# Attention with a memory, then a mixture of experts: loads moved to ScalarE's queue, the sum of the attended values split by head, and a new table of offsets

## The chip, the cores and the metric

The kernel runs on one core of one Trainium2 chip. A core has TensorE (PE: matrix products and transposes, results in eight PSUM banks), VectorE (DVE), ScalarE (ACT), GpSimd (POOL) and SyncE (SP), which mostly issues DMAs. Each engine takes its instructions strictly in the order in which they were written into its queue. The metric is the device time in microseconds of one execution; less is better.

## What is computed

```python
# q, k, v: B=4, H=8, S=576, D=64;  M_prev (B,H,D,D), z_prev (B,H,D), beta (H)
scores = where(causal, -1e9, q @ k^T / sqrt(D));  a = softmax(scores)
local = a @ v
q_p = where(q > 0, q, exp(q) - 1) + 1
mem_out = (q_p @ M_prev) / (q_p . z_prev + 1e-6)
g = sigmoid(beta)                       # one number a head
attn = g * mem_out + (1 - g) * local
x = attn as (B*S, H*D)                  # 2304 tokens x 512
logits = x @ w_gate + modality_bias[modality_id]
e_idx = argmax(logits);  gate_w = softmax(logits)[e_idx]
for e in range(8):                      # F = 1024
    out[e_idx == e] = gate_w * (relu(x @ w1[e]) @ w2[e])
```

Everything is float32.

## The kernel before

A product in float32 accuracy is made of three products of rounded parts: an operand is split into a high part (an `fp32r` copy, by ScalarE) and the rest (value minus copy, by VectorE or GpSimd), so `qh`/`ql`, `kh`/`kl`, `pth`/`ptl`, `vhl`, `xh`/`xl`, `hh`/`hlo`, `w1h`/`w1l` in the traces.

**Attention** goes by pairs of heads (16 pairs, four to a batch of 576 tokens). For a pair: q and k are loaded (`load_t`, `qn`, `kn`), transposed on TensorE (L554), split, and partly copied by DMA to other partitions (`qs`, `ks`, `kls`, L568/L569). Per head: scores on TensorE (L657), mask and row maximum by a VectorE instruction (L669), exponent on ScalarE (L675), transposes (L684), split (L701 ScalarE, L703 VectorE), product with v (L715, L720). A head's attended values stand in PSUM in two halves, partitions 0 to 63 and 64 to 127, that must be added; the function `av` does that into `ot` by way of the buffer `avt`. Then `memory` (L758 to L774: the product with `M_prev`, in the buffer `mz`, loaded by `load_m`), and `combine` (L783 to L801: transposes `ot` back, scales, adds, into the row buffer `xb`, which is stored as x).

**Routing** follows each batch: `gate` makes logits; `route` is a run of small VectorE instructions (steps e0 to e7, L852 to L917) on 128x40 and 128x8 values with three little TensorE products between them, and five indirect DMAs (L920) that GpSimd issues, which scatter (token number, weight) into three tables `tbl`; `rank` (L932 to L945) finds the fullest expert (after batch 0) and the second (after batch 2).

**Experts** work in slots of 256 or fewer rows: `fetch` reads the slot's token numbers from the tables (`idr`, L1009, merged on VectorE, L999/L1000), gathers rows of x by indirect DMA (`xg`, L1016); `slot` transposes them (L1042), makes the first product (L1064), the relu and its split (L1073, L1075), the second product (L1086), scales (L1093) and scatters rows of the output (L1024). `load_w` loads weights (L978) and splits them (L985 ScalarE, L989). The fullest expert's weights are loaded while attention still runs, into the buffers `xg` and `osb`, and three slots of it (EARLY = 3) are run between pairs of the last three batches. `leftovers` lists what the last batch added.

**What sets the order.** No engine chooses at run time. Every step is given to a list scheduler, `Plan`, with its engine, a cost in ns, the buffers it reads and writes and a priority: a number n that counts heads, plus the offset that the table `EARLIER` holds for its stage and engine. Stages are q, k, v, ld (loads), sc (scores), pt (transposes of the probabilities), av, m (memory), c (combine), g, r (route and rank), w (the fullest expert's weights), f and e (its fetches and slots), f1, e1, f2, e2, w1, w2, l, l2 (what follows attention), con (the gate's constants), bet, tab, warm. The scheduler runs its own clock with those costs; among the steps of an engine that could start within `WINDOW` ns of the earliest it emits the one with the lowest priority. A changed cost or offset changes the order of instructions everywhere after it.

The start: TensorE fills the time before data with products of ones (`warm`), q of the first pair is transposed, then k; GpSimd sets up masks and constants; VectorE makes `wgs` and `modf` from the loaded gate constants (L470 to L472) and step e0 of the first routing when the order says so.

## Time and profile before

| what | value |
|---|---|
| median of three runs | 554.32 us (549.8 to 556.81) |
| profiled execution | 550.81 us, its span 549.1 us |
| mean granted clock of TensorE | 0.966 of full speed |
| busy, of the span | PE 497.9 us, DVE 330.5, ACT 329.0, POOL 251.9 |
| DMA traffic, mean | 128 GB/s |

The profiled execution's time is the number that a run reports; the span is what the trace covers of it, 1.7 us less. Shares are of the span. Attention takes about the first 310 us, the last routing is at 337 us, and after it there is almost only TensorE work. "idle before" in a row is how long the engine had nothing running before that instruction, and the name behind the arrow is what its wait ended with.

### The profile page before, as it was taken

The numbers are of one execution on the slowest core, as the hardware profiler recorded it, in microseconds if no ns is written. First come the engines' busy times: TensorE is split into PE (matmuls) and PEld (weight loads), VectorE is DVE, ScalarE is ACT, GpSimd is POOL, SyncE is SP. The second block draws the span as 40 slices with busy tenths as digits, with TensorE's granted clock in tenths as the row PEclk, the third lists the DMA queues.
The fourth block names the chain that finished last, engine by engine and source line by source line (L and its number), as shares of the span: only waits on it lengthen the run. The fifth ranks groups of instructions, "written<-read, shape, count | busy, mean of one in ns | idle before, by whom it ended". The sixth has DMA issues, their size and how long they took to land. (4 is left out here: it accounts for less than half of the span.)

```text
span 549.1 us, 10861 instructions
## 1 busy us (share of the span) xinstructions
PE 497.9 (91%) x3420; PEld 445.1 (81%) x3420; DVE 330.5 (60%) x1066; ACT 329.0 (60%) x923; POOL 251.9 (46%) x257
## 2 busy tenths in 40 slices
PE   8898899987899889979898999769999999999992
PEld 8787888875787778869897898769897987989891
DVE  3788788897798988988878336653315512313010
ACT  4798898986999979979298244333325513222110
POOL 8462984656788768865761062350030004010100
PEclk9799899999899989989899999979999999999997
DMA  5888887988777997953740025474036203000100
GB/s 96 189 206 169 206 201 182 231 189 154 192 176 198 238 189 191 220 164 95 180 110 3 20 61 180 78 233 146 18 96 182 83 19 88 29 19 21 40 0 36
DMA packets 97101, 70.43 MB, mean 128 GB/s; under 512 B 73936, under 2 KB 74320, under 8 KB 97042
## 3 DMA queue, kind: packets, MB, share of 16 engines
q1 hardware_dynamic: 93330, 59.99, 45.2%
q0 software_dynamic: 3712, 9.72, 5.8%
q8 instruction: 28, 0.46, 0.4%
q14 instruction: 31, 0.25, 0.2%
HBM read 32.36 MB, written 10.16 MB: 77 GB/s over the span
## 5 line engine op out<-in xcount | busy, mean ns | idle before, releaser
L675 ACT ACTIVATE P<-P,nm 128x576 f32<-128x576 f32 (+4 forms) x160 | 88.5, 558 | 9.1 <-DVE nm L669 6.0
L1024 POOL DMA_INDIRECT out_dram<-osb,ids x19 | 18.9, 997 | 156.0 <-ACT osb L1093 115.3
L1064 PE MATMUL pa<-xh,w1h 128*128 128x256 f32 (+2 forms) x288 | 84.4, 293 | 2.6 <-ACT xh L1050 2.6
L1064 PE MATMUL pa<-xl,w1h 128*128 128x256 f32 (+2 forms) x288 | 83.4, 290 | 0.5 <-DVE xl L1052 0.3
L1064 PE MATMUL pa<-xh,w1l 128*128 128x256 f32 (+2 forms) x288 | 83.1, 288 | 0.0
L1075 DVE SCALAR_TENSOR_TENSOR hlo<-pa,hh 128x256 fp32r<-128x256 f32 (+1 forms) x72 | 29.8, 416 | 69.8 <-ACT hh L1073 69.7
L703 DVE TENSOR_TENSOR ptl<-pa,pth 128x512 fp32r<-128x512 f32 (+1 forms) x128 | 65.6, 564 | 3.0 <-ACT pth L701 2.4
L1073 ACT ACTIVATE hh<-pa 128x256 fp32r<-128x256 f32 (+1 forms) x80 | 29.0, 367 | 61.1 <-PE pa L1064 54.2
L669 DVE CUSTOM_DVE_ANT_0 P<-pa,maskw 128x320 f32<-128x320 f32 (+3 forms) x160 | 62.2, 427 | 4.2 <-PE pa L657 3.5
L684 PE MATMUL pa<-ident,P 128*128 128x128 f32 x320 | 57.6, 285 | 4.0 <-ACT P L675 3.7
L657 PE MATMUL pa<-ks,qs 128*128 128x192 f32 (+3 forms) x186 | 55.5, 329 | 5.9 <-ACT avt L735 2.9
L1086 PE MATMUL pa<-w2h,hh 128*128 128x512 f32 (+1 forms) x152 | 60.4, 397 | 0.0
L701 ACT ACTIVATE pth<-pa 128x512 fp32r<-128x512 f32 (+1 forms) x128 | 57.0, 511 | 5.0 <-PE pa L684 4.4
L1086 PE MATMUL pa<-w2l,hh 128*128 128x512 f32 (+1 forms) x152 | 59.6, 392 | 0.0
L1064 PEld LDWEIGHTS pa<-xh,w1h 128*128 128x128 f32 x288 | 55.6, 193 | 3.4 <-ACT xh L1050 2.9
L1064 PEld LDWEIGHTS pa<-xl,w1h 128*128 128x128 f32 x288 | 55.6, 193 | 1.2 <-DVE xl L1052 0.9
L1086 PE MATMUL pa<-w2h,hlo 128*128 128x512 f32 (+1 forms) x144 | 56.5, 392 | 0.0
L1064 PEld LDWEIGHTS pa<-xh,w1l 128*128 128x128 f32 x288 | 55.5, 193 | 0.0
L1093 ACT ACTIVATE osb<-pa,ids 128x512 f32<-128x512 f32 (+1 forms) x19 | 13.1, 687 | 68.4 <-PE pa L1086 63.1
L657 PE MATMUL pa<-kls,qs 128*128 128x192 f32 (+3 forms) x186 | 49.2, 295 | 0.4 <-DMA kls<-kl 0.4
L684 PEld LDWEIGHTS pa<-ident,P 128*128 128x128 f32 x320 | 40.4, 147 | 6.3 <-ACT P L675 6.0
L684 PE MATMUL pa<-swp,P 128*128 128x128 f32 x160 | 39.5, 287 | 6.1 <-DVE kl L617 2.5
(234 smaller groups left out, 1198.9 us busy)
## 6 DMA issues: line engine op xcount, KB each, us to landing
ks<-kh SPq DMA_DIRECT2D x62, 144.0 KB, 3.0
kls<-kl SPq DMA_DIRECT2D x62, 144.0 KB, 3.4
raw<-in_moe_w_dram SPq DMA_DIRECT2D x32, 256.0 KB, 3.5
qn<-in_q_dram SPq DMA_DIRECT2D x32, 144.0 KB, 4.3
kn<-in_k_dram SPq DMA_DIRECT2D x32, 144.0 KB, 4.2
qs<-qh SPq DMA_DIRECT2D x31, 144.0 KB, 2.6
qs<-ql SPq DMA_DIRECT2D x31, 144.0 KB, 2.7
vn<-in_v_dram SPq DMA_DIRECT2D x32, 128.0 KB, 3.0
```

Source lines behind the costliest of these rows:

```text
L657: nc.tensor.matmul(t.ap[0:m, o:o + z - x], lhsT=l[:, QS[j]:QE[j]], rhs=r[:, x:z], start=(i == 0), stop=(i == len(terms) - 1))
L669: nc.vector.tensor_tensor_reduce(out=pj[:, x:z], in0=t.ap[0:m, o:o + z - x], in1=mk, scale=-1.0, scalar=nm if x else 3.0e38, op0=ALU.add, ...
L675: g.op("ACT", act_ns(w, False, 2), lambda pj=pj, nm=nm, den=den, w=w: nc.scalar.activation(out=pj[:, 0:w], in_=pj[:, 0:w], func=AF.Exp, sc ...
L684: nc.tensor.transpose(t[:, o:o + P], prow[c % NPB][j][:, kb * P:(kb + 1) * P], swp if j == kb else ident)
L701: g.op("ACT", act_ns(n), lambda t=t, o=o, n=n: nc.scalar.activation(out=hi[:, o:o + n], in_=t.ap[:, 0:n], func=AF.Copy), r=[t], w=[("ph_", ...
L703: g.op("DVE", dve_ns(n), lambda t=t, o=o, n=n: nc.vector.tensor_tensor(out=lo[:, o:o + n], in0=t.ap[:, 0:n], in1=hi[:, o:o + n].bitcast(F3 ...
L1024: g.op("POOL", 1310, lambda: nc.gpsimd.indirect_dma_start(out=out[:, :], out_offset=bass.IndirectOffsetOnAxis(ap=ids[u % 4][0:m, t, 0:1].b ...
L1064: nc.tensor.matmul(hp.ap[:, 0:n_], lhsT=a[:, c, f * P:(f + 1) * P], rhs=x_[:, c, 0:n_], start=(n == 0), stop=(n == 3 * KC - 1))
L1073: g.op("ACT", act_ns(z - a), lambda f=f, hp=hp, i=i, a=a, z=z: nc.scalar.activation(out=hh[i][:, f, 0:z - a], in_=hp.ap[:, a:z], func=AF.R ...
L1075: g.op("DVE", dve_ns(z - a), lambda f=f, hp=hp, i=i, a=a, z=z: nc.vector.scalar_tensor_tensor(out=hlo[i][:, f, 0:z - a], in0=hp.ap[:, a:z] ...
L1086: nc.tensor.matmul(op.ap[0:m], lhsT=a[:, f, ts], rhs=w_[:, f], start=(y == 0 and n == 0), stop=(y == 3 and n == 5))
L1093: g.op("ACT", act_ns(512, True, 1), lambda t=t, op=op, oi=oi: nc.scalar.activation(out=osb[oi][0:m], in_=op.ap[0:m], func=AF.Copy, scale=i ...
```

## The change

It has three parts. First, the loads of the first pair's v, of the first batch's memory (`M_prev`, `z_prev`) and of beta are issued from ScalarE's queue instead of SP's. Second, in `av`, the two heads of a pair are treated differently: for head 0 ScalarE copies both halves of the attended values and GpSimd adds them; for head 1 ScalarE copies the lower half and VectorE adds the upper half to it straight from PSUM. Before, both heads of every even pair went the first way and both heads of every odd pair went the second way (there ScalarE copied the upper half). The copy always stands in partitions 0 to 63 of `avt` now. Over the kernel each way is taken as often as before. Third, the planner's costs of some steps are raised (e0 1150 to 1700 ns, e7 600 to 750, rank 1000 to 2700, two steps of the leftovers, the adds and copies of `av`), the last five heads and the three early slots get stages of their own in the table, and all offsets and windows are new.

```diff
     NPR = B * NP
-    Plan.WINDOW = dict(zip(("PE", "ACT", "DVE", "POOL", "SP"), (0, 80, 85, 135, 75)))
+    Plan.WINDOW = dict(zip(("PE", "ACT", "DVE", "POOL", "SP"), (5, 45, 105, 0, 115)))

     EARLIER = {
-        "av": (-240.75, -614.75, 695.5, -837, 0),
-        "bet": (0, 0, 0, 0, -366),
-        "c": (-412, 0, 147.25, -2057.75, 0),
...
-        "con": (0, 0, 0, 0, -347.25),
-        "m": (418, 232, 747.75, 90.5, 0),
-        "warm": (-247, 0, 0, 0, 0),
...
+        "av": (-315.5, -552, 201.5, -507, 0),
+        "av9": (-136.25, -579.75, 581, -194.75, 0),
+        "bet": (0, -180, 0, 0, 0),
+        "con": (0, 0, 0, 0, -125),
+        "fa": (0, 0, 1223.5, 412.75, 556),
+        "m": (550.75, 31.5, 1031, 63.75, 0),
+        "m9": (341, -318.75, 1001.5, 260.25, 0),
+        "warm": (-3, 0, 0, 0, 0),
...
-        g.op("SP", emit=lambda: nc.sync.dma_start(out=bet, in_=beta.unsqueeze(0).to_broadcast([P, H])), w=["bet"],
+        g.op("ACT", emit=lambda: nc.scalar.dma_start(out=bet, in_=beta.unsqueeze(0).to_broadcast([P, H])), w=["bet"],
...
         b, h0 = divmod(p * 2, H)
         t, keys = nat[nm][p % len(nat[nm])], [(nm, p % len(nat[nm]))]
         s2 = src[b, h0:h0 + 2]
+        other = nm == "v" and p == 0
+        q_ = nc.scalar if other else nc.sync

         def e():
             if nm != "v":
                 for j in range(2):
-                    nc.sync.dma_start(out=t[0:TP, :, j], in_=s2[j].rearrange("(t p) d -> p t d", p=TP))
+                    q_.dma_start(out=t[0:TP, :, j], in_=s2[j].rearrange("(t p) d -> p t d", p=TP))
                 return
             for j in range(2):
-                nc.sync.dma_start(out=t[:, 0:4, j], in_=s2[j, 0:512, :].rearrange("(c p) d -> p c d", p=P))
-            nc.sync.dma_start(out=t[0:64, 4], in_=s2[:, 512:576, :].rearrange("h p d -> p h d"))
-
-        g.op("SP", emit=e, w=keys, prio=prio, **dma_ns(*([(525, 610), (525, 610), (700, 150)] if nm == "v" else [(625, 666)] * 2)))
+                q_.dma_start(out=t[:, 0:4, j], in_=s2[j, 0:512, :].rearrange("(c p) d -> p c d", p=P))
+            q_.dma_start(out=t[0:64, 4], in_=s2[:, 512:576, :].rearrange("h p d -> p h d"))
+
+        g.op("ACT" if other else "SP", emit=e, w=keys, prio=prio, **dma_ns(*([(525, 610), (525, 610), (700, 150)] if nm == "v" else [(625, 666)] * 2)))

     def load_m(b, prio):
-        m = mz[b % 2]
+        m, q_ = mz[b % 2], nc.sync if b else nc.scalar

         def e():
             for j in range(2):
-                nc.sync.dma_start(out=m[64 * j:64 * j + 64, :, j, 0:D],
+                q_.dma_start(out=m[64 * j:64 * j + 64, :, j, 0:D],
                                   in_=M_prev[b].rearrange("(p j) d e -> j d p e", j=2)[j])
-                nc.sync.dma_start(out=m[64 * j:64 * j + 64, :, j, D],
+                q_.dma_start(out=m[64 * j:64 * j + 64, :, j, D],
                                   in_=z_prev[b].rearrange("(p j) d -> j d p", j=2)[j])

-        g.op("SP", emit=e, w=[("mz", b % 2)], prio=prio, **dma_ns(*[(625, 364), (625, 112)] * 2))
+        g.op("SP" if b else "ACT", emit=e, w=[("mz", b % 2)], prio=prio, **dma_ns(*[(625, 364), (625, 112)] * 2))
...
-        o_, a_ = ot[p % 2][64 * hh:64 * hh + 64], avt[0][64 * hh:64 * hh + 64]
+
+        o_, a_ = ot[p % 2][64 * hh:64 * hh + 64], avt[0][0:64]
         for part, (t, a, z) in enumerate(((ta, 0, P), (tb, P, S))):
             n, ko = z - a, ("ot", p % 2, hh, part)
-            if d % 4 < NAVP:
+            if hh == 0:
                 g.op("ACT", act_ns(n), lambda t=t, a=a, z=z, n=n: nc.scalar.activation(
                     out=o_[:, a:z], in_=t.ap[0:64, 0:n], func=AF.Copy), r=[t], w=[ko], prio=prio)
-                g.op("ACT", act_ns(n), lambda t=t, a=a, z=z, n=n: nc.scalar.activation(
+                g.op("ACT", act_ns(n) + 180, lambda t=t, a=a, z=z, n=n: nc.scalar.activation(
                     out=a_[:, a:z], in_=t.ap[64:P, 0:n], func=AF.Copy), r=[t], w=[("avt", part)], prio=prio)
             else:
                 g.op("ACT", act_ns(n), lambda t=t, a=a, z=z, n=n: nc.scalar.activation(
-                    out=avt[0][0:64, a:z], in_=t.ap[64:P, 0:n], func=AF.Copy), r=[t], w=[("avt", part)], prio=prio)
-                g.op("DVE", dve_ns(n), lambda t=t, a=a, z=z, n=n: nc.vector.tensor_tensor(
-                    out=o_[:, a:z], in0=t.ap[0:64, 0:n], in1=avt[0][0:64, a:z], op=ALU.add),
+                    out=a_[:, a:z], in_=t.ap[0:64, 0:n], func=AF.Copy), r=[t], w=[("avt", part)], prio=prio)
+                g.op("DVE", dve_ns(n) + 110, lambda t=t, a=a, z=z, n=n: nc.vector.tensor_tensor(
+                    out=o_[:, a:z], in0=t.ap[64:P, 0:n], in1=a_[:, a:z], op=ALU.add),
                      r=[t, ("avt", part)], w=[ko], prio=prio)
-        if d % 4 < NAVP:
+        if hh == 0:
             g.op("POOL", 1420, lambda: nc.gpsimd.tensor_tensor(out=o_, in0=o_, in1=a_, op=ALU.add),
                  r=[("avt", 0), ("avt", 1)], w=[("ot", p % 2, hh, 0), ("ot", p % 2, hh, 1)], prio=prio)
...
-        g.op("DVE", 1150, e0, w=["l0", "l1", "pr", "eb"], r=["basec", "modf", "iote", "tid"], prio=prio)
+        g.op("DVE", 1700, e0, w=["l0", "l1", "pr", "eb"], r=["basec", "modf", "iote", "tid"], prio=prio)
...
-        g.op("DVE", 600, e7, r=["rex"], w=["sx", "pr"], prio=prio)
+        g.op("DVE", 750, e7, r=["rex"], w=["sx", "pr"], prio=prio)
...
-        g.op("DVE", 1000, e, r=["basec"], w=["nst"] + ([("perm", 0)] if b == 0 else []) +
+        g.op("DVE", 2700, e, r=["basec"], w=["nst"] + ([("perm", 0)] if b == 0 else []) +
...
+        def at(stage):
+            return stage + ("9" if n >= NH - 5 else "")
+
         if 0 <= n < NH:
-            av(n, ("av", n))
+            av(n, (at("av"), n))
         if 0 <= n + 1 < NH:
-            ptrans(n + 1, ("pt", n))
+            ptrans(n + 1, (at("pt"), n))
...
-                            fetch(g, b, start(b), 2, ["nst", ("perm", 0)], ("f", n), (b + 1) * S)
-                            slot(g, b, 0, 2, ("e", n))
+                            fetch(g, b, start(b), 2, ["nst", ("perm", 0)], ("f" + "abc"[b], n), (b + 1) * S)
+                            slot(g, b, 0, 2, ("e" + "abc"[b], n))
...
-    attn = [o for o in g.ops if o.stage not in ("r", "w", "f", "e")]
+    attn = [o for o in g.ops if o.stage[:1] not in set("rwfe")]
...
     steps = leftovers()
-    for i, ns in enumerate((2200, 1400, 2600, 2600)):
+    for i, ns in enumerate((2800, 1750, 2600, 2600)):
         g.op("DVE", ns, lambda: next(steps), r=["basec", "thr", "swap"] + (["left"] if i else []),
```

What the new table does to the queues is seen in the order of the instructions. The first place is VectorE at the start, from the first split of k on, before (`modi`: the modality numbers as loaded, `P`: the masked scores, `nm`: their negated maxima):

```order
L617 TENSOR_TENSOR kl_147<-pa_93,kh_146 128x288
L617 TENSOR_TENSOR kl_147<-pa_94,kh_146 128x288
L596 SCALAR_TENSOR_TENSOR ql_145<-pa_92,qh_144 128x288
L669 ISA P_4_163,nm_169<-pa_95,maskw 128x320
L669 ISA nm_169 128x1
L669 ISA P_1_160,nm_169<-pa_95,maskw 128x192
L669 ISA nm_169 128x1
L669 ISA P_4_163,nm_169<-pa_96,maskw,nm_169 128x256
```

and VectorE after, from the first split of k on:

```order
L630 TENSOR_TENSOR kl_147<-pa_93,kh_146 128x288
L630 TENSOR_TENSOR kl_147<-pa_94,kh_146 128x288
L481 CAST wgs<-wg 128x4x8
L482 TENSOR_TENSOR wgs<-wg,wgs 128x4x8
L483 CAST modf<-modi 128x20
L866 TENSOR_TENSOR l_125<-modf,bias_73 128x40
L867 TENSOR_SCALAR l_126<-modf 128x40
L868 TENSOR_TENSOR l_126<-l_126,bias_73 128x40
L869 TENSOR_TENSOR l_126<-l_126,l_125 128x40
L870 TENSOR_SCALAR pr<-tid 128x5
L871 TENSOR_TENSOR eb<-basec,eoff 128x8
L682 ISA P_4_163,nm_169<-pa_95,maskw 128x320
```

The work on the gate's constants and step e0 of the first routing, nine instructions that stood behind the first head's masks, now stand ahead of the first mask.

ScalarE at the same place, before, from the last copies of q on:

```order
L583 ACTIVATE qh_144<-pa_92 128x288
L585 ACTIVATE ex_148<-pa_92 128x288
L615 ACTIVATE kh_146<-pa_93 128x288
L615 ACTIVATE kh_146<-pa_94 128x288
L588 ACTIVATE ph_149<-pa_92 128x288
L675 ACTIVATE P_1_160,nden<-P_1_160,nm_169 128x192
```

and after:

```order
L596 ACTIVATE qh_144<-pa_92 128x288
L598 ACTIVATE ex_148<-pa_92 128x288
L601 ACTIVATE ph_149<-pa_92 128x288
L538 DMA mz_176<-in_M_prev_dram 64x4x64
L540 DMA mz_176<-in_z_prev_dram 64x4x1
L538 DMA mz_176<-in_M_prev_dram 64x4x64
L540 DMA mz_176<-in_z_prev_dram 64x4x1
L628 ACTIVATE kh_146<-pa_93 128x288
L628 ACTIVATE kh_146<-pa_94 128x288
L688 ACTIVATE P_1_160,nden<-P_1_160,nm_169 128x192
```

Four loads of the memory are issued between the copies of q and the copies of k (`kh`). The loads of beta and v stand at the head of ScalarE's queue.

The second place is ScalarE around the first of the fullest expert's weights (`w1h` is the high part, `xg` the buffer they were loaded into), before:

```order
L615 ACTIVATE kh_146<-pa_93 128x288
L701 ACTIVATE pth_171<-pa_91 128x512
L701 ACTIVATE pth_171<-pa_96 128x512
L701 ACTIVATE pth_171<-pa_92 128x512
L701 ACTIVATE pth_171<-pa_95 128x64
L985 ACTIVATE w1h_98<-xg_108 128x512 x2
L733 ACTIVATE ot_174<-pa_91 64x128
L735 ACTIVATE avt_173<-pa_91 64x128
```

and after:

```order
L714 ACTIVATE pth_171<-pa_92 128x512
L688 ACTIVATE P_4_163,nden<-P_4_163,nm_169 128x576
L714 ACTIVATE pth_171<-pa_93 128x512
L714 ACTIVATE pth_171<-pa_91 128x512
L714 ACTIVATE pth_171<-pa_92 128x64
L688 ACTIVATE P_0_159,nden<-P_0_159,nm_169 64x64
L688 ACTIVATE P_3_162,nden<-P_3_162,nm_169 128x448
L999 ACTIVATE w1h_98<-xg_108 128x512
L752 ACTIVATE avt_173<-pa_96 64x128
```

The first two copies of weights stood directly behind the split of a head's probabilities; now one copy stands there, behind four more instructions of the next heads, among them the exponents of `P_0_159` and `P_3_162`. VectorE makes their masks here, `rank` ending with the cast to `nsti`, after:

```order
L954 CAST nsti<-nst 128x8
L609 SCALAR_TENSOR_TENSOR ql_145<-pa_95,qh_144 128x288
L682 ISA P_4_163,nm_169<-pa_91,maskw 128x320
L682 ISA nm_169 128x1
L682 ISA P_1_160,nm_169<-pa_91,maskw 128x192
L682 ISA nm_169 128x1
L609 SCALAR_TENSOR_TENSOR ql_145<-pa_92,qh_144 128x288
L797 SCALAR_TENSOR_TENSOR rnd<-nden,gg 128x10
L799 RECIPROCAL rnd<-rnd 128x10
L682 ISA P_4_163,nm_169<-pa_97,maskw,nm_169 128x256
L682 ISA nm_169 128x1
L630 TENSOR_TENSOR kl_147<-pa_93,kh_146 128x288
```

(the masks of `P_0_159` and `P_3_162` follow as rows 14 and 16 behind the cast).

The third place is GpSimd at the last routing, before (`tbl_61` to `tbl_63` are the three tables):

```order
L801 TENSOR_TENSOR xb_182<-xb_182,mt_181 128x5x128
L920 DMA tbl_61<-pr,dst 18432x2
L920 DMA tbl_62<-pr,dst 18432x2
L1024 DMA out_dram<-osb_113,ids_103 2304x512
L920 DMA tbl_63<-pr,dst 18432x2
L920 DMA tbl_61<-pr,dst 18432x2
L920 DMA tbl_62<-pr,dst 18432x2
L1024 DMA out_dram<-osb_113,ids_103 2304x512
L1016 DMA xg_4300<-x_dram,ids_105 128x512 x2
```

and after:

```order
L815 TENSOR_TENSOR xb_182<-xb_182,mt_181 128x5x128
L934 DMA tbl_61<-pr,dst 18432x2
L934 DMA tbl_62<-pr,dst 18432x2
L934 DMA tbl_63<-pr,dst 18432x2
L934 DMA tbl_61<-pr,dst 18432x2
L934 DMA tbl_62<-pr,dst 18432x2
L1038 DMA out_dram<-osb_113,ids_103 2304x512
L1030 DMA xg_4272<-x_dram,ids_105 128x512 x2
```

The store of output rows that stood between the second and the third scatter now stands behind the fifth.

## Rows read from the trace of the kernel before

**Rows 1.** The profile page: busy times, and TensorE's clock in 40 equal slices

```profile
PE 497.9 (91%) x3420; PEld 445.1 (81%) x3420; DVE 330.5 (60%) x1066; ACT 329.0 (60%) x923; POOL 251.9 (46%) x257
...
PEclk9799899999899989989899999979999999999997
```

**Rows 2.** Windows: span, length, busy time of each engine, granted clock, DMA share, GB/s

```profile
3.00:6.00 3.00, 3.00 (x31) 3.00 (x29) 0.19 (x1) 0.31 (x2) 2.88 (x19) 1.00 1.17 237
28.00:42.00 14.00, 13.15 (x97) 11.75 (x95) 11.56 (x41) 13.27 (x41) 8.97 (x8) 1.00 0.84 208
126.00:140.00 14.00, 9.74 (x63) 7.76 (x62) 9.53 (x41) 9.07 (x24) 8.01 (x7) 0.98 0.81 163
200.00:205.00 5.00, 4.79 (x26) 4.49 (x27) 3.44 (x12) 3.43 (x12) 1.95 (x2) 0.66 0.68 149
270.00:275.00 5.00, 5.00 (x36) 4.92 (x35) 3.17 (x11) 1.34 (x4) 4.63 (x4) 0.74 0.30 68
392.00:420.00 28.00, 28.00 (x176) 24.18 (x175) 9.89 (x26) 10.82 (x25) 6.10 (x6) 1.00 0.30 90
```

**Rows 3.** Timeline of the start, VectorE, TensorE and SP's queue

```profile
10.79 0.49 DVE L669 CUSTOM_DVE_ANT_0 P<-pa,maskw 128x320 f32<-128x320 f32 x1 [0.94 <-PE pa L657]
...
13.73 1.16 DVE L472 CAST modf<-modi 128x20 f32<-128x20 int32 x1
...
15.69 0.16 DVE L857 TENSOR_TENSOR eb<-basec,eoff 128x8 f32<-128x8 f32 x1
...
18.87 0.51 PE L657 MATMUL pa<-ks,qs 128*128 128x192 f32 x1
...
9.61 2.50 SPq L467 DMA_DIRECT2D modi<-in_moe_modality_id_dram  x4
...
16.03 0.64 SPq L525 DMA_DIRECT2D mz<-in_M_prev_dram  x1
```

**Rows 4.** Timeline around the fullest expert's first weights: VectorE, SP, ScalarE, TensorE

```profile
128.31 0.17 DVE L940 CAST nsti<-nst 128x8 int32<-128x8 f32 x1
...
129.28 0.92 SPq L978 DMA_DIRECT2D xg<-in_moe_w_dram  x2
...
135.23 1.40 ACT L985 ACTIVATE w1h<-xg 128x512 fp32r<-128x512 f32 x2 [4.59 <-DMA xg<-in_moe_w_dram]
...
137.26 0.38 PE L657 MATMUL pa<-ks,qs 128*128 128x256 f32 x1 [2.90 <-ACT avt L735]
```

**Rows 5.** Waits from 25 to 300 us: total, times, longest

```profile
PE pa L794 <- POOL ot L744: 1.6, 3, 0.7
```

**Rows 6.** Timeline: one routing instruction twice, GpSimd beside the first, two of TensorE's waits

```profile
195.43 2.51 DVE L906 TENSOR_TENSOR l<-l,oh 128x40 f32<-128x40 f32 x1
...
263.81 0.20 DVE L906 TENSOR_TENSOR l<-l,oh 128x40 f32<-128x40 f32 x1
...
196.48 1.39 POOL L603 TENSOR_TENSOR ph<-ph,ex 128x576 f32<-128x576 f32 x1
...
149.86 0.71 PE L554 MATMUL pa<-ident,qn 96*128 96x96 f32 x6 [1.53 <-DVE kl L617]
...
269.07 1.07 PE L794 MATMUL pa<-ident,ot 128*128 128x128 f32 x4 [2.27 <-DVE ot L740]
```

**Rows 7.** Timeline of the last routing: TensorE, GpSimd, SP's queue

```profile
337.61 0.27 PE L898 MATMUL pa<-ohb,ones 128*128 128x8 bf16 x5
...
348.48 0.39 PE L1064 MATMUL pa<-xh,w1h 128*128 128x256 f32 x1 [2.62 <-ACT xh L1050]
...
362.13 0.45 PE L1042 MATMUL pa<-ident,xg 128*128 128x128 f32 x1 [3.25 <-issue]
364.03 1.75 PE L1042 MATMUL pa<-ident,xg 128*128 128x128 f32 x7 [1.46 <-DMA xg<-x_dram,ids]
...
346.26 0.98 POOL L920 DMA_INDIRECT tbl<-pr,dst  x1 [0.31 <-DMA tbl<-pr,dst]
...
353.92 3.29 SPq L1009 DMA_DIRECT2D idr<-tbl  x6
```

65 lines of the change are left out of this document (37 added, 28 removed).

## The prediction

> **What bounds the kernel now.** I read the page first: TensorE is busy for 497.9 of 549.1 us and every other engine for 60% or less, so TensorE is the bound of the whole, and some 51 us of its idle time are what an order of instructions can win; the other thing to win is its clock, which the row of slices shows below full speed in many slices of attention and at full speed in nearly all of the second half [rows 1]. The windows then say where the idle time lies. From 392 to 420 us TensorE is busy without a gap at full clock, so nothing that the change does to the expert stage can shorten that stage [rows 2]. From 28 to 42 us, in attention, TensorE has 13.15 of 14 us, ScalarE 13.27 and VectorE 11.56: there two engines are full and a third nearly so [rows 2]. A new order can't make such a stretch much shorter; it can only take away the places where the flow breaks. From 126 to 140 us it breaks: 9.74 of 14 us [rows 2]. The timelines of these places name who ended the waits: the start [rows 3], the first weights [rows 4], the ends of pairs [rows 5], the routing steps on VectorE [rows 6] and the last routing [rows 7]. The six terms below are made against the profiled execution, 550.81 us, whose span is 549.1. The median of the runs is 554.32, so a result of the sum is multiplied by 554.32/550.81 = 1.0064 at the end.
>
> **The start.** Before, the first mask begins on VectorE at 10.79 us and the constants of the gate follow, ending at 15.85 [rows 3]. Now these constants and step e0 come first, and the cast of `modi` can't start before its last load has landed. SP's four loads of `modi` end at 12.11, each some 0.6 us, and the cast began at 13.73 [rows 3]; with beta gone from SP's queue I put the landing at 13.2 to 13.7. From the cast's start to the end of e0 the trace has 15.85 - 13.73 = 2.1 us, of which the cast's 1.16 may shrink. The first mask so begins at about 14.6 to 15.8, 3.8 to 5 us late. Part of that comes back, since the constants no longer stand behind the masks, and the next step of TensorE that starts at 18.87, the second head's scores, needs copies by DMA that are issued as before [rows 3]. The end at which all is hidden is -0.5 (SP is freed of one issue), the other is +5. I take **+2.5**, the middle, because TensorE's work on the first head's probabilities has to fit between the late masks and that point. The four memory loads cost SP some 0.64 us each [rows 3], so 2.5 us of ScalarE if they cost the same there, in front of the copies of k and of all exponents behind them. Here they cost nothing, because VectorE waits longer for `modi`; without that cover they would cost those 2.5 us. The load of v moves nothing on the path, since q and k stand first in SP's queue either way.
>
> A rule speaks against a gain from the other queue. The row: from 3 to 6 us the transfers keep the DMA engines full (share 1.17, 237 GB/s) [rows 2]. The Trainium skill, "DMA: Bandwidth & Descriptors", section "Issuing engines are not separate DMA queues", says that transfers started by different engines run on the same 16 DMA engines and interleave, and that a second issuer saves only issue time. The row agrees that the resource is full. By it, v's bytes, now issued beside those of q and k, would delay these: 288 KB at 237 GB/s are 1.2 us, and the sum would be -4.6 in place of -5.8.
>
> **The first weights.** Before, ScalarE came to the first copy of weights 4.59 us before they had landed; it held back the copies of the attended values, and TensorE stood still for 2.90 us [rows 4]. The weights landed 135.23 - 128.48 = 6.75 us after the cast that ends `rank` (the load is issued at 129.28) [rows 4]. Now the copy stands behind two exponents whose masks are the 14th and the 16th row of VectorE behind that cast. Those sixteen rows (masks of 0.49 for 320 columns, as at 10.79 [rows 3], and splits of the same order) make about 5.2 us, the exponent some 0.8 more, so ScalarE comes to the copy at 6.0 and waits 0.75 instead of 4.59. Of TensorE's 2.90 us I leave 0.8: **-2.1**, between -2.9 and 0 (the load stands behind other transfers).
>
> **The ends of pairs.** TensorE waited three times, 1.6 us in all, for GpSimd's sum of attended values [rows 5]. On an even pair GpSimd did two such adds one after the other, now one, and on an odd pair one in place of none. The counts of copies and adds are the same on every engine, so their busy time doesn't change. I take half, **-0.8**; the ends are -1.6 and, if odd pairs now wait as even ones did, +1.6.
>
> **The last routing.** From the counts' matmul at 337.61 to the arrival of the new slot's rows at 364.03 it is 26.4 us, in which TensorE stands still for 2.62 + 3.25 + 1.46 = 7.3 us [rows 7]. The chain is: counts, five scatters (the last issued at 346.26), landing, SP's fetch at 353.92, merge, gather [rows 7]. The store that leaves the row of scatters takes 0.98 us and a gap of 0.30 like the scatter shown, so the chain falls to about 25.1. TensorE's cover, between 337.61 and 362.13, was 24.5 - 5.9 - 0.3 = 18.3 us for 30 products of the second kind, 84 of the first and 8 transposes. After the change 42 and 96 stand there, 138 in place of 122, by that ratio 20.7 us. What is left is 4.4 us of idle time: **-2.9**. The ends: -7.3 (cover enough) and +2.6 (the store that now comes five scatters later holds ScalarE's output buffer, so that the 2.62 us come a second time).
>
> **The routing steps on VectorE.** The same instruction of 128x40 takes 0.20 us at 263.81 and 2.51 us at 195.43; the second ends within 0.1 us of a GpSimd multiplication of 1.39 us that began at 196.48 and that followed another one without a gap [rows 6]. TensorE waits behind such held steps five times, the first 1.53 us and the last 2.27, together 8.1 us [rows 6]. The raised costs of e0, e7 and `rank` let the planner put other work beside them, but nothing in it knows that GpSimd holds them, so which of them are hit is drawn anew. I take **-1.5**, near no change; the ends are -8.1 and +8.1.
>
> **The clock.** Behind two of these waits the granted clock of the next 5 us is 0.66 and 0.74 [rows 2], which is 1.7 and 1.3 us of work lost while the lower of the two levels, 1.2 GHz, lasts. With fewer long waits I take **-1**, from -3 to 0.
>
> **Sum:** +2.5 - 2.1 - 0.8 - 2.9 - 1.5 - 1 = -5.8, so 545.0, times 1.0064: **548.5 us**. Its own range, by the ends of the terms that are independent, is 542 to 554.
>
> **The rivals.** *The holds go as well.* If the new order keeps GpSimd's tensor work away from the routing steps, the term is -8.1 and the clock's -3: -14.4, so 536.4 and 540 us. For it: it takes a shift of 2 us at five places. Against: no offset is tied to it. *Only reshuffled.* In a stage where ScalarE and VectorE are full [rows 2], a wait that goes from one engine comes back at the next full one; then the start alone counts: +2.5, 553.3, 557 us. For it: 13.27 of 14 us on ScalarE. Against: the breaks at 126 to 140 and at the last routing lie where engines are not full. *Slower: the holds double.* GpSimd now adds at the end of every pair, odd ones too, and its window in the planner is 0, so its tensor work stands closer together. If twice as many routing steps run beside it, TensorE idles 8.1 us more, its clock dips twice more (3 us), the start adds 2.5, and the other gains go under: +13.6, 564.4, 568 us. It is slower by 2% once the sum is over +11, that is, from 5.5 us of new waits behind held steps on. For it: the 2.51 against 0.20 us. Against: the number of GpSimd's tensor instructions is the same. The Trainium skill, "SBUF — State Buffer", section "Who interferes with whom", states this mechanism: a VectorE instruction with two inputs in SBUF contends with a GpSimd instruction that reads SBUF, and one of them is fully blocked. The 2.51 us of the instruction with two such inputs agrees.
>
> **How the numbers follow.** The forecast has 0.50, the lost holds 0.18, the reshuffle 0.20, the doubled holds 0.12. A measurement of this kernel tells about 2% from no change, so faster means under 543.2 and slower over 565.4. Faster: most of the second case (0.16) and the low end of the first (0.08), 0.24. Slower: two thirds of the last, 0.08. The rest, 0.68, is within 2%. The range of 8 in 10 takes in the forecast's own and the reshuffle, and half of each outer case: 537 to 561.
>
> **What would show it.** In the changed kernel's trace: the first mask at 14.6 to 15.8 us; ScalarE's wait for the first weights under 1.5 us and TensorE's wait there gone; between the counts of the last routing and the new slot's rows idle time near 4.4 us; some held steps of 1 to 2.5 us on VectorE at new places; TensorE without a gap in the expert stage. It would be wrong above all if those held steps are gone or doubled, if the late masks shift all of attention by 4 us or more, or if the full engines give each gain back one stage later.

## The result, and the profile after

Measured together, the changed kernel takes 555.81 us (median of 20 runs, 553.21 to 558.9) and the kernel before 550.21 (546.04 to 556.98): ratio 1.0123, 95% interval 1.0099 to 1.0146. The ratio is taken over runs in the faster of the chip's two states alone, so it isn't the quotient of the two medians, which is 1.0102. The change makes the kernel 1.2% slower by the ratio, where 1.0% faster was forecast. The profiled execution after takes 558.59 us, its span is 556.9, its mean granted clock 0.961. It is 2.8 us above the median of its kernel and that of before 0.6 above, so by the medians some 2 of the 7.8 us between the two spans belong to these two executions and not to the change.

The page after, busy times and TensorE's clock:

```profile
PE 503.5 (90%) x3420; PEld 448.8 (81%) x3420; DVE 332.7 (60%) x1066; ACT 323.8 (58%) x923; POOL 250.6 (45%) x257
...
PEclk9599999999889997898999999999999999999998
```

Against [rows 1] the span grows by 7.8 us. TensorE is busy 5.6 us longer with the same 3420 products and idle 2.2 us longer. So most of the loss is not a longer wait but the same work going slower. The mean clock accounts for 3.0 us of it (0.039 of 556.9 less 0.034 of 549.1, an estimate); the other 2.6 us of busy time I can't name. The two lowest slices after are the second, which shows 5 (14 to 28 us), and the 16th, 7 (209 to 223 us); before they show 7 and 9.

To see where, I compared how much TensorE has done by a given time in each trace, every product counted at the lower quartile of the spacings of its kind. I call what after stands behind before the lag. It is an estimate, good to some 2 us: its last value should come out at the 7.8 us between the spans. The lag is 3.5 us of work at 40 us, 2.8 at 200, 10.1 at 220, 10.6 at 240, 14.8 at 260, 10.7 at 300, 14.3 at 340, 9.9 at 360 and about 9.5 from 400 on. So the losses lie at the start, from 200 to 220 and from 240 to 260. What 240 to 260 loses is given back by 300 us; 3.6 us are lost again from there to 340, the last routing gives 4.4 back, and the expert stage is only shifted.

**The start**, timeline of VectorE, TensorE, ScalarE's queue (ACTq) and ScalarE:

```profile
14.58 0.18 DVE L483 CAST modf<-modi 128x20 f32<-128x20 int32 x1 [1.81 <-DMA modi<-in_moe_modality_id_dram]
...
15.63 0.48 DVE L682 CUSTOM_DVE_ANT_0 P<-pa,maskw 128x320 f32<-128x320 f32 x1
...
19.08 0.50 PE L670 MATMUL pa<-kls,qs 128*128 128x192 f32 x1 [1.32 <-DMA kls<-kl]
...
22.64 1.11 PE L697 MATMUL pa<-ident,P 128*128 128x128 f32 x4
...
7.79 0.63 ACTq L538 DMA_DIRECT2D mz<-in_M_prev_dram  x1
...
10.40 0.60 ACTq L540 DMA_DIRECT2D mz<-in_z_prev_dram  x1
11.05 0.71 ACT L628 ACTIVATE kh<-pa 128x288 fp32r<-128x288 f32 x2 [3.04 <-DMA mz<-in_M_prev_dram]
```

VectorE waits for the modality numbers, so the first mask comes at 15.63 instead of 10.79 [rows 3]. The first transposes of probabilities come at 22.64; before they came at

```profile
12.31 0.33 PE L684 MATMUL pa<-ident,P 128*128 128x128 f32 x1
14.56 0.90 PE L684 MATMUL pa<-ident,P 128*128 128x128 f32 x3 [1.92 <-ACT P L675]
```

The late masks are not the only reason: in TensorE's new order the second head's scores (L670, from 17.23 us on) and the transposes of the next k stand ahead of these transposes. On ScalarE's queue the fourth memory load goes out 2 us after the issue of the third has ended, for a reason that no run shows, and the copy of k behind it waits 3.04 us. The windows at the start, after (the granted clock is the third column from the end):

```profile
14.00:20.00 6.00, 4.68 (x20) 3.76 (x18) 3.58 (x20) 3.57 (x13) 0.61 (x1) 0.50 0.96 216
20.00:26.00 6.00, 5.17 (x27) 5.03 (x27) 3.69 (x14) 4.22 (x13) 5.66 (x6) 0.53 0.65 141
```

and before:

```profile
20.00:26.00 6.00, 5.78 (x46) 5.27 (x45) 3.76 (x17) 5.29 (x17) 2.46 (x3) 1.00 0.92 223
```

The lower level, 1.2 GHz, lasts about 6 us longer.

**The first weights**, timeline of VectorE, SP's queue, ScalarE, TensorE:

```profile
132.76 0.23 DVE L954 CAST nsti<-nst 128x8 int32<-128x8 f32 x1
...
133.41 1.01 SPq L528 DMA_DIRECT2D vn<-in_v_dram  x2
134.51 1.22 SPq L529 DMA_DIRECT2D vn<-in_v_dram  x1
136.73 0.93 SPq L992 DMA_DIRECT2D xg<-in_moe_w_dram  x2
...
143.08 0.63 ACT L999 ACTIVATE w1h<-xg 128x512 fp32r<-128x512 f32 x1 [3.65 <-DMA xg<-in_moe_w_dram]
...
144.47 0.55 PE L697 MATMUL pa<-ident,P 128*128 128x128 f32 x3 [3.29 <-ACT P L688]
```

The three loads of one pair's v now stand between the cast and the weights' load. The weights are there 10.3 us after the cast began, not 6.9 [rows 4], and the waits are as before.

**From 204 to 225 us**, timeline of VectorE, GpSimd and TensorE:

```profile
212.31 6.00 DVE L797 SCALAR_TENSOR_TENSOR rnd<-nden,gg 128x10 f32<-128x10 f32 x1 [2.29 <-ACT P L688]
218.34 0.22 DVE L799 RECIPROCAL rnd<-rnd 128x10 f32<-128x10 f32 x1
...
211.81 1.40 POOL L758 TENSOR_TENSOR ot<-ot,avt 64x576 f32<-64x576 f32 x1 [0.77 <-ACT avt L749]
213.18 1.29 POOL L1003 TENSOR_TENSOR w2l<-osb,w2h 128x512 fp32r<-128x512 f32 x1
214.44 2.49 POOL L1003 TENSOR_TENSOR w2l<-xg,w2h 128x512 fp32r<-128x512 f32 x2
216.89 1.39 POOL L616 TENSOR_TENSOR ph<-ph,ex 128x576 f32<-128x576 f32 x1
...
219.25 0.33 PE L697 MATMUL pa<-swp,P 128*128 128x128 f32 x1 [3.40 <-DVE nm L682]
```

One step of `combine` on ten numbers a partition takes 6.00 us. It starts in the first of five GpSimd instructions that follow one another without a gap and ends 0.03 us behind the last. The masks stand behind it, and TensorE waits 3.40 us for them. The windows there:

```profile
215.00:220.00 5.00, 1.39 (x11) 0.96 (x10) 4.96 (x11) 1.54 (x3) 3.28 (x3) 1.00 0.52 118
220.00:225.00 5.00, 4.86 (x19) 4.14 (x18) 4.71 (x17) 3.92 (x14) 0.00 (x0) 0.53 0.93 258
```

TensorE has 1.39 of 5 us and then works 5 us at 0.53. A second such place:

```profile
249.19 2.77 DVE L869 TENSOR_TENSOR l<-l,l 128x40 f32<-128x40 f32 x1
...
249.12 1.40 POOL L758 TENSOR_TENSOR ot<-ot,avt 64x576 f32<-64x576 f32 x1 [0.62 <-ACT avt L749]
250.48 1.43 POOL L815 TENSOR_TENSOR xb<-xb,mt 128x640 f32<-128x640 f32 x1
251.88 1.26 POOL L1003 TENSOR_TENSOR w2l<-xg,w2h 128x512 fp32r<-128x512 f32 x1
```

This step ends with the second of three GpSimd instructions in a row. TensorE waits 2.67 us behind it, and has 1.97 us of work from 250 to 255.

**The last routing**, timeline of TensorE, GpSimd and SP's queue:

```profile
346.63 0.27 PE L912 MATMUL pa<-ohb,ones 128*128 128x8 bf16 x5
...
368.41 0.39 PE L1078 MATMUL pa<-xh,w1h 128*128 128x256 f32 x1 [3.12 <-DVE w1l L1003]
...
372.85 0.98 PE L1056 MATMUL pa<-ident,xg 128*128 128x128 f32 x7 [1.25 <-DMA xg<-x_dram,ids]
...
353.60 0.97 POOL L934 DMA_INDIRECT tbl<-pr,dst  x1 [0.32 <-issue]
...
361.27 3.30 SPq L1023 DMA_DIRECT2D idr<-tbl  x6
```

Idle time between the counts and the new rows falls from 7.3 [rows 7] to 4.4 us. TensorE's clock stays up there, in the window after:

```profile
365.00:370.00 5.00, 1.88 (x16) 1.68 (x15) 3.57 (x10) 1.18 (x3) 3.76 (x4) 1.00 0.76 213
```

while behind the same place before it was 0.68:

```profile
365.00:370.00 5.00, 5.00 (x26) 4.72 (x25) 3.25 (x6) 2.35 (x6) 2.42 (x3) 0.68 0.79 219
```

### The profile page after: what moved, and what is told of

The parts are those of the page before. It is cut to its first block, busy times and chain, and to the rows that moved or that the text cites. A ratio compares the mean times of both kernels' runs of the same rounds, so it can differ in the third digit from the quotient of the medians.

```text
span 556.9 us, 10879 instructions
## 1 busy us (share of the span) xinstructions
PE 503.5 (90%) x3420; PEld 448.8 (81%) x3420; DVE 332.7 (60%) x1066; ACT 323.8 (58%) x923; POOL 250.6 (45%) x257
## 5 line engine op out<-in xcount | busy, mean ns | idle before, releaser
L670 PE MATMUL pa<-ks,qs 128*128 128x192 f32 (+3 forms) x186 | 59.3, 344 | 2.7 <-DMA qs<-ql 0.8
L670 PE MATMUL pa<-kls,qs 128*128 128x192 f32 (+3 forms) x186 | 51.6, 306 | 1.3 <-DMA kls<-kl 1.3
```

Of the source, the lines that this page charges most:

```text
L670: nc.tensor.matmul(t.ap[0:m, o:o + z - x], lhsT=l[:, QS[j]:QE[j]], rhs=r[:, x:z], start=(i == 0), stop=(i == len(terms) - 1))
```

## The experiments

Ratios are to the kernel before, which ran beside each. My theory (T1 in the expectations) was that the broken places, the held step and the late start above all, make the loss; its rival (T2) that what one such place costs or gives is given back in the stages behind it. An expectation words them for its own run.

### The held step

**c4_no_hold_212.** In the one combine that was held for 6.00 us, ScalarE makes the product.

```diff
+            if p in (10,):
+                for h in range(2):
+                    nc.scalar.activation(out=rnd[:, :, h:h + 1], in_=nden[:, p % 4, :, h:h + 1], func=AF.Copy,
+                                         scale=gg[:, 0, 0, h0 + h:h0 + h + 1])
+                nc.vector.reciprocal(out=rnd, in_=rnd)
+                return
```

> The changed kernel with its planned order kept, but for one pair (the eleventh) ScalarE multiplies the denominators by the gate (two small instructions) in place of the one VectorE instruction that took 6.00 us while GpSimd ran five tensor instructions in a row. Theory 1: VectorE goes on at 213 us, TensorE's wait of 3.40 us at 219 and the half clock behind it go, 4 to 7 us are won, ratio 1.000 to 1.005. Theory 2: the wait goes, but the time comes back before the last routing, ratio 1.010 to 1.013. If another VectorE instruction with two operands in SBUF is held in its place, the wait stays, 1.012.

Measured 1.0046 (1.0015 to 1.0076); the interval lies under that of the change. In its profile the 6.00 us are gone and the clock from 220 to 230 us is 1.00, but the next pair's step is held instead, by another row of five:

```profile
241.26 6.79 DVE L803 SCALAR_TENSOR_TENSOR rnd<-nden,gg 128x10 f32<-128x10 f32 x1
```

TensorE waits 6.23 us there in that execution (557.56 us, above this kernel's median of 555.8). So the gain is measured, but the profile shows that the fault can move; this run alone doesn't price the hold.

**c7_products_on_gpsimd.** The products of all pairs go to GpSimd, where they queue behind its own work.

```diff
-            nc.vector.scalar_tensor_tensor(out=rnd, in0=nden[:, p % 4], scalar=1.0e-9,
-                                           in1=gg[:, 0, :, h0:h0 + 2].to_broadcast([P, NB, 2]), op0=ALU.add, op1=ALU.mult)
+            nc.gpsimd.tensor_tensor(out=rnd, in0=nden[:, p % 4],
+                                    in1=gg[:, 0, :, h0:h0 + 2].to_broadcast([P, NB, 2]), op=ALU.mult)
...
```

The product `rnm` in `memory` changes likewise. The small numbers added to both before are left out.

> The changed kernel with its planned order kept, but for all pairs the product of denominators and gate (rnd) and of the memory's norm and gate (rnm) is made by one small GpSimd instruction each, and VectorE keeps only the reciprocals (the added 1e-9 and 1e-6 are left out). The run before had shown that one such step freed at 212 us gives another that is held for 6.8 us at 241. Theory 1 (VectorE, held by rows of GpSimd's tensor work, makes the extra loss in attention): no rnd or rnm step over 0.6 us is left, the stretch 200 to 255 us loses 4 to 8 us less, ratio 0.998 to 1.004; the held steps of the routing stay. Theory 2 (the loss comes back in full stages): 1.010 to 1.013. Theory 3: the products come late, behind other GpSimd work, and VectorE waits for them as long as before: 1.008 to 1.016.

Measured 1.0041 (1.0007 to 1.0075). The step is gone, and so is the dip from 215 to 225 us:

```profile
215.00:220.00 5.00, 4.71 (x40) 4.22 (x38) 4.81 (x18) 5.00 (x18) 4.76 (x8) 1.00 0.94 253
220.00:225.00 5.00, 4.54 (x34) 4.05 (x33) 2.76 (x8) 4.91 (x17) 4.00 (x5) 1.00 0.93 230
```

The lag at 220 us is 3.6 instead of 10.1. The wait for the first weights is gone here as well, so c7's gain isn't the held step's alone; c4 and c10 keep that wait (2.56 and 2.64 us). A step e0 of the routing remains held for 2.62 us at 244.41, and TensorE waits 3.55 behind it.

**c10_splits_on_vector.** Here VectorE keeps the step; three splits of weights leave GpSimd's row of five.

```diff
-            g.op(lo, 1220 if lo == "POOL" else dve_ns(512), lambda i=i, t=t, e=nc.gpsimd if lo == "POOL" else nc.vector:
+            g.op(lo, 1220 if lo == "POOL" else dve_ns(512), lambda i=i, t=t, e=nc.gpsimd if lo == "POOL" and i not in (11, 12, 13) else nc.vector:
```

> The changed kernel with its planned order kept, but three of GpSimd's splits of weights, those that stood at 213 to 217 us in the row of five under which one VectorE step took 6.00 us, are made by VectorE, in place; the rnd step itself stays. Theory 1 (the row of GpSimd's work holds VectorE): the step at 212 shrinks to under 3 us though VectorE has three more instructions of 0.69 us, TensorE's wait of 3.40 behind it falls under 1.5, ratio 1.003 to 1.009. Theory 2 (won here, lost behind): the step shrinks and the ratio stays at 1.010 to 1.014. If the 6 us were something else than GpSimd's row, the step stays at 6.

Measured 1.0052 (1.0019 to 1.0085). With two GpSimd instructions in the row, the same step is held until the second of them ends:

```profile
213.16 2.60 DVE L797 SCALAR_TENSOR_TENSOR rnd<-nden,gg 128x10 f32<-128x10 f32 x1 [1.21 <-ACT P L688]
...
212.96 1.41 POOL L758 TENSOR_TENSOR ot<-ot,avt 64x576 f32<-64x576 f32 x1
214.33 1.39 POOL L616 TENSOR_TENSOR ph<-ph,ex 128x576 f32<-128x576 f32 x1
...
216.69 0.33 PE L697 MATMUL pa<-swp,P 128*128 128x128 f32 x1 [1.35 <-DVE nm L682]
```

At this place the hold follows the length of GpSimd's row, and TensorE's wait falls from 3.40 to 1.35. So the row is what holds the step there, shown from GpSimd's side. The clock dips here all the same, to 0.51 from 220 to 225 us in a profile of this kernel's slowest run (557.08), so this trace doesn't show where the gain lies.

**c5_e0_on_gpsimd** and **c14_products_and_e0.** The first puts e0 of the last three batches on GpSimd, the second adds the products as in c7.

```diff
+            v = nc.gpsimd if b in (1, 2, 3) else nc.vector
```

> The changed kernel with its planned order kept, step e0 of the routing alone on GpSimd from the second batch on; the rnd step held for 6 us at 212 stays. Theory 1: 3 to 5 us less lost at 245 to 260 us, ratio 1.003 to 1.008. Theory 2: 1.010 to 1.014.

> The changed kernel with its own start and planned order; the products of c7 and step e0 of the routing from the second batch on are made by GpSimd. In c7 and c12 an e0 step held for 2.6 us near 245 us still left TensorE waiting 3.5 us and its clock low behind it. Theory 1 (held steps are the loss beside the start): the stretch 240 to 260 us loses 3 to 5 us less than in c7, ratio 0.996 to 1.001. Theory 2 (lost again before the end): as c7, 1.002 to 1.007, and the trace shows where.

Measured 1.0093 (1.0055 to 1.0131) and 1.0054 (1.0024 to 1.0084). e0 alone isn't told apart from the change; a hold of 6.27 us at 211.29 stays there. With both no step is held over 1.8 us, yet it is no faster than c7. That doesn't make e0's hold worthless, since in this profile a wait of 4.44 us stands at the same place:

```profile
247.49 0.38 PE L670 MATMUL pa<-ks,qs 128*128 128x192 f32 x1 [4.44 <-DMA idr<-tbl]
```

The two runs were measured beside each other and differ by the products alone: 0.4%, with intervals that overlap.

**b1_before_with_products.** The edits of c14 (products and e0) in the kernel before, whose longest hold is 2.51 us [rows 6].

> The kernel before, its planned order kept, with rnd, rnm and e0 on GpSimd. If the held steps cost it what its trace shows (2.40 us at 146.7, 1.25 and 1.33 at 234.5 to 237, 0.93 at 238.9, with 1.5, 1.0 and 1.2 us of TensorE's waits; the 2.51 at 195 and the 2.15 at 265 are other steps and stay), theory 1 gives 3 to 5 us, ratio 0.991 to 0.996. Theory 2: 1.000. Theory 3: 1.002 to 1.01.

Measured 0.9985 (0.9951 to 1.002): no gain that can be told, though up to 0.5% would lie in the interval. The held steps that these edits take away were 2.40 us and shorter; the one of 2.51 us is another step and was not moved.

### The start

In these, the planner makes its order as in the change, and tagged steps are emitted later.

**c1_memory_late.** The first memory goes back to SP, behind v of the second pair, and the second memory's loads behind q of the fifth pair.

```diff
-        m, q_ = mz[b % 2], nc.sync if b else nc.scalar
+        m, q_ = mz[b % 2], nc.sync
...
```

> The changed kernel with its planned order kept, but the four loads of the first memory go back to SP's queue, behind the load of the second v (the second batch's memory, which stood there, is issued behind the fifth pair's q). Theory 1 (the loss has places: the start, 3 to 4 us, and the steps that GpSimd holds near 212 and 249 us): the copies of k start at about 8.1 us in place of 11.05, but the first mask still waits for the constants, to 14.5 or later, so under 1.5 us are won, ratio to the kernel before 1.009 to 1.013. Theory 2 (a win at one place is lost again in the full stages behind it): 1.012. Theory 3 (the issue of the memory's loads on ScalarE is the whole loss at the start): first mask near 12.5 us, ratio 1.006 or less.

Measured 1.0103 (1.0058 to 1.0148), the first mask still at 15.85. The loads that hold up ScalarE cost nothing that can be told while VectorE waits for the constants; its interval reaches down to 1.0058, so a gain of some 0.6% isn't excluded.

**c2_constants_late** and **c3_start_as_before.** The constants and the first e0 behind head 0's six masks; in c3 both edits.

```diff
-        g.op("DVE", 500, consts2, r=["wg", "modi"], w=["wgs", "modf"], prio=3)
+        g.op("DVE", 500, consts2, r=["wg", "modi"], w=["wgs", "modf"], prio=3).tag = "late"
...
```

> The changed kernel with its planned order kept, but VectorE makes the gate's constants and step e0 of the first routing behind the six masks of the first head, as in the kernel before; the memory's loads stay on ScalarE. Theory 1: the first mask starts at about 12.6 us in place of 15.63, 2 to 3 us are won, ratio 1.006 to 1.009. Theory 2: 1.012. Theory 3: the masks still start late, 1.011 or more.

> Both of these edits together, so that the start runs as in the kernel before. Theory 1: first mask at 10 to 11 us, the stretch of half clock at the start ends by 20 us in place of 25, 3.5 to 5 us are won, ratio 1.003 to 1.006, and the held step of 6 us near 210 us is still there. Theory 2: the first mask comes as early, but the ratio stays at 1.010 to 1.013.

Measured 1.0093 (1.0061 to 1.0125) and 1.0088 (1.0059 to 1.0118). Neither is told apart from the change. The first mask comes at 13.32 and 10.73, but TensorE can't use it, since its order after has the second head's scores ahead of the first head's transposes. In c3, a window and two rows of TensorE:

```profile
14.00:20.00 6.00, 1.59 (x4) 1.00 (x4) 2.49 (x11) 2.45 (x8) 2.33 (x2) 0.63 0.95 211
...
16.58 0.50 PE L684 MATMUL pa<-ks,qs 128*128 128x192 f32 x1 [3.63 <-DMA ks<-kh]
...
21.76 1.11 PE L711 MATMUL pa<-ident,P 128*128 128x128 f32 x4
```

**c11_start_with_tensor_order.** c3, and TensorE's order at the start as before too.

```diff
+            if not self.gone and (o.tag in ("hold", "hold1") or o.deps & self.hold.keys() or any(
+                    k is not x and k.at == x.at and k.n == x.n for h in self.hold for x in h.slots for k in o.slots)):
+                self.hold[o] = None
...
```

The transposes of q and k of the second piece and the second head's scores carry the tag, and are let go with the first head's transposes.

> The edits of c3 (memory's loads on SP behind the first copies, constants behind the masks) and the order that the kernel before has on TensorE at the start: the transposes of the first head's probabilities ahead of the second pair's q, of the second head's scores and of the second pair's k, with what hangs on these on the other engines; from there on the changed kernel's planned order. If the order of TensorE's first steps carries the rest of the start's loss (theory 1): TensorE's wait of 3.6 us for the copies of k that c3 still has at 14 to 20 us goes, 2 to 4 us are won on c3, ratio 1.001 to 1.006. Theory 2 (what is won at the start is lost in the full stages behind it): as c3, 1.007 to 1.011.

Measured 1.0123 (1.0064 to 1.0181). The lag is 1.3 us at 30 us, but 3.2 at 40 and 5.2 at 80:

```profile
26.00:40.00 14.00, 11.77 (x89) 10.36 (x88) 9.24 (x30) 10.25 (x31) 7.24 (x8) 1.00 0.85 208
40.00:60.00 20.00, 15.92 (x119) 13.67 (x117) 14.20 (x51) 17.40 (x55) 12.62 (x11) 1.00 0.82 186
```

TensorE has 11.77 us of 14 and 15.92 of 20, after the change it had 12.48 and 17.40. What the start wins is lost right behind it, as T2 has it. Whether full engines take it back or the steps that were held back themselves, this run doesn't tell.

**b2_late_start.** The reverse in the kernel before: only the memory loads on ScalarE ahead of the copy of k, and the constants and e0 ahead of the masks.

```diff
+            for x in self.ops if o.tag in ("mask", "kh") else ():
+                if x.tag == {"mask": "con", "kh": "mem"}[o.tag] and x.emit:
+                    x.emit()
+                    x.emit = None
...
```

> The kernel before, its planned order kept, but with the changed kernel's start on two engines: the four loads of the first memory on ScalarE ahead of the copies of k, the gate's constants and e0 on VectorE ahead of the first head's masks. Theory 1 (what the start loses is lost for good): first mask at 14.5 to 15.8 us, 2.5 to 4 us lost, ratio 1.004 to 1.008. Theory 2 (a loss is made good in the stages behind it): 0.998 to 1.002.

Measured 1.0104 (1.005 to 1.0158). The first mask comes at 17.35, later than after the change, and

```profile
10.00:14.00 4.00, 0.49 (x2) 0.49 (x3) 0.51 (x2) 0.96 (x3) 3.26 (x3) 0.89 0.35 25
```

TensorE has almost nothing from 10 to 14 us. The lag is 4.2 at 40 us and in its profile grows at the last routing from 7.8 (360 us) to 11.1 (400 us). So a late start can cost 1% by itself, in the old order; but this one is worse than that of the change, where TensorE works from 11.52 us on. In the new order it could not be undone.

### The first weights, and several at once

**c9_weights_first.** c7, with the weights' first three loads ahead of the loads of v.

```diff
+            if o.tag == "v":
+                self.held = o
+            else:
+                o.emit()
+            if o.tag == "w2":
+                self.held.emit()
...
```

> The edit of c7, and the first three loads of the fullest expert's weights are issued ahead of the ninth pair's v, which waited for its buffer on SP's queue and kept them to 136.73 us, 3.7 us behind the cast that ends rank. Theory 1: the weights land some 2 to 3 us earlier, ScalarE's wait of 3.65 us and TensorE's of 3.29 at 144 us fall under 1.5, ratio 0.998 to 1.002. Theory 2: as c7, 1.004.

Measured 1.0048 (1.0014 to 1.0082). ScalarE's copy starts at 140.22 without a wait and TensorE's wait is gone. But c7's own profile has neither wait (its copy starts at 141.80), so this run had nothing left to win there and doesn't price the wait.

**c8_products_and_start** (c3, c7 and e0 on GpSimd), **c12_start_and_products** (c11 and c7) and **c13_and_weights_first** (c12 and the loads of c9):

> The edits of c7 and of c3 (start as before), and step e0 of the routing from the second batch on, on GpSimd. Theory 1: the gains add: 2 us at the start, 4 to 8 from rnd and rnm, 2 to 3 from e0: ratio 0.992 to 1.000, as fast as the kernel before or faster. Theory 2: 1.006 to 1.010, that is c3 alone. Theory 3: 1.008 or more.

> c11 and the products of c7 on GpSimd, without the e0 step of c8. Theory 1 (two places, the start and the held steps, and their gains add): 1.0123 less 0.006 for the start and 0.008 for the steps, ratio 0.994 to 1.002. Theory 2: no better than c7, 1.003 to 1.008.

> c12 with the first three loads of the fullest expert's weights ahead of the ninth pair's v, as in c9, where this took away ScalarE's and TensorE's wait and won nothing. Theory 1: 0.990 to 1.001, a version as fast as the kernel before or faster. Theory 2: as c12.

Measured 1.0069 (1.0037 to 1.0102), 1.0121 (1.0053 to 1.0188) and 1.0065 (1.002 to 1.0111). None beats c7 alone, so no sum of gains shows. c12's runs go from 551.43 to 563.85, too wide to place it.

Set side by side, the new orders in which the step at 212 us is still held for 6 us lie at 1.0088 to 1.0123 (the change, c1, c2, c3, c5, c11), those in which it isn't at 1.0041 to 1.0069 (c4, c7, c8, c9, c10, c13, c14) and, too wide, c12 at 1.0121. Against the ranges set down before each run, T1 came out in c1, c4, c7 (at its edge) and c10, T2 in c8, c9, c14 and b1; c2, c3, c5 and c13 fell between the two, and c11, c12 and b2 were slower than both.

### Parts of the change alone

**b_av_by_head** (the sums by head, with the old table) and **b_loads_on_scalar** (the loads on ScalarE's queue, with the old table); the planner was free to reorder.

```diff
-            if d % 4 < NAVP:
+            if hh == 0:
...
```

> The kernel before with only the sum of the attended values split by head (head 0 by GpSimd, head 1 by VectorE), its costs and offsets as before; the planner sets the order anew. If this split is what makes GpSimd stand longer beside VectorE (rival of the prediction: adds at the end of every pair): ratio 1.01 or more with more held rnd steps in the trace. If the split is neutral and the loss comes with the table: 0.997 to 1.006.

> The kernel before with only the first part of the change: beta, the first v and the first memory loaded from ScalarE's queue; its own costs and offsets (but for beta's, which is the new one), so that the planner sets the order anew. If these loads alone cost the start what it lost (theory 1 with the loads as the cause): ratio 1.004 to 1.010. If they are neutral and the place of the constants is the cause: 0.997 to 1.003. A new order can bring other waits, as the split by head alone showed.

Measured 1.0671 (1.0629 to 1.0713) and 1.0589 (1.0533 to 1.0645). TensorE's waits from 330 to 420 us in b_av_by_head:

```profile
PE pa L1042 <- issue: 22.6, 1, 22.6
```

At the end of attention (300 us) it is not behind before by the lag, and its held steps lose about as much; one stall at the last routing makes most of the loss. The other has one of 14.5 us there and was already some 15 to 18 us behind at 300 us. So its 1.0671 is not the rival's doubled holds, and the other's 1.0589 lies far over its forecast. They price the table, which fits one set of steps only, not the parts; what either part costs in a fitted order stays open.

## Why the prediction was wrong

The terms, forecast and as the trace after has them:

| term | forecast, us | found, us |
|---|---|---|
| start | +2.5 | +3.5 of lag at 40 us |
| first weights | -2.1 | +0.4 (2.90 to 3.29) |
| ends of pairs | -0.8 | -1.2 (1.6 to 0, and 0.4 new behind L754) |
| last routing | -2.9 | -2.9 (7.3 to 4.4) |
| held steps | -1.5 | +1.2 (8.1 to 1.01 + 2.19 + 3.40 + 2.67 = 9.3) |
| clock | -1 | +3.0 over the span |

They overlap (the start's lag holds some of the clock) and make 4.0 of the 7.8 us of the two profiles; the rest I can't lay to one place.

**The step that failed** is the pair "routing steps" and "clock", forecast near no change: -1.5 and -1, found +1.2 and +3.0. The mechanism was named in the prediction, as the rival "the holds double", but its size was read off five waits, as holds of 1 to 2.5 us, the length of one or two GpSimd instructions. The holds together didn't grow much: over all steps VectorE loses about 24 us before and 26 after, counted above the median length of each kind of step (an estimate).

But one step was held by a row of five, TensorE waited 3.40 us for it, and behind that the clock stood at 0.53 for 5 us: from 200 to 220 us the lag grows by 7.3 us, of which 2.19 + 3.40 us are waits. Three different edits that free this step or shorten its hold (c4, c7, c10) bring the kernel to 1.0041 to 1.0052. That is 0.7 to 0.8% under the change's own ratio, and 0.4 to 0.6% under c1 to c3, which keep the hold and ran beside c4; none of the three edits changes this place alone (c7 also loses the wait for the first weights). It also lay at a step of `combine`, while the prediction spoke of routing steps only.

What is left without the hold, 1.0041 to 1.0052, is what the rival "only reshuffled" forecast (553.3 against 550.81, 1.0045). c11, where a start won early was lost again by 80 us, points the same way. That full engines are the reason is argued, not shown.

By the Trainium skill, "SBUF — State Buffer", section "Who interferes with whom", whichever starts first holds the shared ports for its whole instruction and the other is blocked until it ends. The blocking agrees; by the letter the step should have started 0.9 us later, when the first GpSimd instruction ended (213.2). It was let in at 218.3, behind all five. Other held steps did get in between (the last section), so the row's end is no rule.

**First weights.** This term failed by a queue that the prediction had walked past: on SP the loads of a pair's v now stand ahead of the weights. It had given the end 0 for that case and taken -2.1. What this wait is worth no run shows, since c7, against which c9 is read, doesn't have it.

**The start.** The size was near, +3.5 for +2.5, but the reason was in part another: the prediction took TensorE to work on the first head's probabilities ahead of the second head's scores, as before, and the new order has them behind. In c3 the masks are back at 10.73 us, and the transposes still come at 21.76.

**Right:** the first mask (14.6 to 15.8 forecast, 15.63 found); the memory loads hidden on ScalarE, as far as c1's interval tells; the idle time of the last routing, though by two errors that cancel: cover and chain were both longer than forecast (the chain 26.2 us in place of 25.1), and the waits that remain end with VectorE's split `w1l` first, then with the gather. Its clock gain, 0.68 to 1.00, was not forecast. The expert stage has no gap from 392 to 420 us, as said. Of the 1.2 us by which v's bytes might have delayed those of q and k, TensorE shows a wait of 0.26 us for q's load at 5.61 us and none for k's, whose transposes stand behind products of ones until 8.26.

**Open:** the other 0.4 to 0.5%. The late start is a candidate (b2), and so is the reshuffling itself, but no run took the late start out of the new order without losing the time again. Nothing tried beats the kernel before.

## What to carry to other kernels

Before an order is judged by its waits, look for the longest row of GpSimd tensor instructions without a gap and for which two-input VectorE step falls into it, since it can be held to the row's end: one step of ten numbers a partition cost 6 us of VectorE and 0.4 to 0.8% of this kernel. Price a TensorE wait with the clock behind it: 3.40 us idle came with 5 us at 0.53, and in c10 1.35 us with 5 us at 0.51. And undoing one move in a table that was fitted as a whole may win nothing (c2, c3, c11).

## What was not expected of the hardware

The product step of `combine` at 212 us was not let in between GpSimd instructions that follow one another: 6.00 us behind five (also 6.01 to 6.27 in c1, c2, c3, c5 and c11), 2.60 behind two in c10; the one at 241 us in c4 took 6.79. Elsewhere a held step was let in: the e0 step at 249.19 ended at 251.96, when the second of three GpSimd instructions was over (251.91) and the third had begun (251.88), and in c10 the product step itself at 245.51 took 0.98 us, with the next GpSimd instruction already begun. What decides it no run shows. Steps with one tensor input were held too, if less often:

```profile
188.83 1.31 DVE L894 TENSOR_SCALAR oh<-l 128x40 f32<-128x40 f32 x1
```

as long as the 1.4 us of the GpSimd add beside it (188.7). And a DMA issued on ScalarE held up its arithmetic: the fourth memory load, itself issued late, at 10.40 us, kept the copy of k idle for 3.04 us.
